# Order of loads, transposing DMAs and TensorE items in a fused sliding-window attention and MLP kernel

## The chip, the cores and the metric

The kernel runs on one core of one Trainium2 chip. The metric is the device time of one execution in microseconds. The kernel before was run four times: 331.54, 331.69, 332.9 and 333.54 us, median 332.3 us.

## What is computed

Attention with 8 batches, 8 heads, 576 positions and head size 64, in float32 at the kernel's inputs. Each query sees itself and the 127 keys before it, with a linear distance bias that depends on the head. Its output, as 4608 tokens of 512 values, goes through a two-layer MLP (512 to 2048 to 512) with the activation h / (1 + exp(-beta h)).

```python
scores = scale * np.matmul(q, k.transpose(0, 1, 3, 2))
bias = slopes[:, None, None] * (-np.abs(rel).astype(np.float32))[None, :, :]
mask = (rel >= 0) & (rel < window)          # window 128
scores = np.where(mask, scores + bias[None], -1000000000.0)
attn = softmax(scores)                      # with 1e-09 in the divisor
x = matmul(attn, v) as tokens               # (8 * 576, 512)
h = x @ w_in
g = h * (1.0 / (1.0 + np.exp(-beta * h)))
out = g @ w_out
```

## The kernel before, in words

All matmuls are in bfloat16. The work comes in small steps, each a function.

Attention, for batch b: a batch has five blocks of queries or keys (four of 128 rows and a tail of 64), and its heads go in four pairs p. For batches 0 to 2, `load_pair` (L101) brings q and k of two heads from HBM to `fst` tiles (SP's queue, L109) and GpSimd casts them into a `bst` tile (L113); `load_tail` (L117) does the same for the last 64 rows of all heads (loads L95, casts L119). `TP` and `TT` (L220, L234) transpose these on TensorE into the tile `qkT`. For batches 3 to 7, `load_qk` (L123) brings one block of q and k for all heads (loads L95 on SP, casts L129 on GpSimd) and `TD` (L245) transposes it with two transposing DMAs on SP's queue (L248). `load_v` (L134) brings a block of v: for batches 0 to 2 a load on SP and a cast (L142), for later ones a casting DMA that GpSimd issues (L137). `SC(b, m, p)` (L257) forms the scores of a pair in one half m and their exponentials (matmuls L285, ScalarE L293 or L298, VectorE mask L302). Half m = 0 needs key blocks 0 and 1 (queries up to row 383), half 1 the other three. `PV(b, qb, g)` (L314) multiplies with v for four heads of query block qb (L325, L329) and divides (VectorE L334, L335), into the tile `xn`. `X(b, qb)` (L341) puts the block, transposed, into the tile `XT`, a ring of 1536 tokens: by TensorE and a copy for batches 0 to 2 (L353, L358), by a transposing DMA on SP's queue for later ones (L349).

MLP, in nine groups g of 512 tokens: `HS(g, j)` (L363) makes one of 16 blocks of hidden values (four matmuls L372, ScalarE tanh L377, VectorE L378, into the tile `gT`); `OS(g, i, n)` (L382) adds a quarter n of the second product for 128 tokens i (four matmuls L388); with n = 3 it also scales the result on ScalarE (L403) and queues the store, which GpSimd issues two items later (L406). Below, H items and O items are calls of these.

TensorE's order is written out by hand. Batch 0 comes first; `by_pair(b)` lists the steps of batches 1 and 2, `by_block(b)` those of batches 3 to 7. `spread(moe, todo, lead, goals)` calls the list `moe` of H and O items one by one and the attention steps `todo` between them, in even measure, from item `lead` on. Batch 1 (list `s1`) runs beside group 0's items 6 to 15, batch 2 (list `s2`) beside groups 0 and 1, and later batches beside group g's H items, which alternate with the O items of group g-1 and the first three of group g.

SP's and GpSimd's orders follow from program order too. For batches 2 to 7 `merge` sets it: it gives each load, cast, TD, v load and each X of batches 3 to 7 (the list `lazy`) a place among TensorE's steps, and sorts. `first[b]` is the place of batch b's first step. A queue works in order: an instruction that waits holds those behind it. SP's queue holds loads, TD and X; GpSimd's holds casts, v loads and stores.

Of the kernel before, what the change touches and what calls it, by code (L numbers as in the profile page):

```python
# [17 lines left out]
def kernel(  # L18
# [28 lines left out]
    NTG = T // TOKG  # L47
# [69 lines left out]
    def load_tail(b):  # L117
        for i, src in enumerate((q, k)):
            nc.gpsimd.tensor_copy(  # L119
                out=tails[b % 2][0 : S - LM, i], in_=load_rows(src, b, NQB - 1)  # L120
            )
# [307 lines left out]
    def spread(moe, todo, lead, goals):  # L429
        sums = [0]  # L430
        for f in todo:
            sums.append(sums[-1] + cost.get(f, 0))
        goals = [(m, sums[n]) for m, n in goals]
        m0, w0, k = lead, 0, 0
        slope = None
        for i, it in enumerate(moe):
            flush()
            it()
            while goals and (slope is None or i + 1 >= m1):

                if slope is not None:
                    m0, w0 = m1, w1
                    goals = [g for g in goals if g[0] > m0]
                    if not goals:
                        break
                slope, m1, w1 = max(((w - w0) / (m - m0), m, w) for m, w in goals)
            w = w0 + slope * (i + 1 - m0)
            while k < len(todo) and (sums[k] + sums[k + 1]) / 2 <= min(w, w1):
                todo[k]()
                k += 1  # L450
        for f in todo[k:]:
            f()

    def step(f, c):
        cost[f] = c
        return f
# [17 lines left out]
    def pv(b, qb, g):  # L474
        return step(lambda: PV(b, qb, g), 1)
# [12 lines left out]
    def merge(steps, first):  # L488
        jobs = []

        def vals(b, sb, t0):
            casts = []
            jobs.append((t0, lambda: casts.append(load_v(b, sb))))
            if b < NTE:
                jobs.append((t0 + 4.5, lambda: casts.pop()()))

        for sb in range(NQB):
            vals(NTE - 1, sb, 1.5 * sb)
        for b in range(NTE, B):
            for sb in range(NQB):  # L500
                casts = []
                t0 = first[b] - 25 + 4.6 * sb
                jobs.append((t0, lambda b=b, sb=sb, c=casts: c.append(load_qk(b, sb))))
                jobs.append((t0 + 4.5, lambda c=casts: c.pop()()))
                jobs.append((t0 + 8.5, lambda b=b, sb=sb: TD(b, sb)))
                vals(b, sb, first[b] - 16 + 3 * sb)
        for i, f in enumerate(steps):
            if f in lazy:
                jobs.append((i + 2, f))
        jobs.sort(key=lambda j: j[0])  # L510
        out = []
        for i, f in enumerate(steps):
            while jobs and jobs[0][0] <= i:
                out.append(jobs.pop(0)[1])
            if f not in lazy:
                out.append(f)
        return out + [j[1] for j in jobs]
# [39 lines left out]
    with tc.manual_schedule(engines={mybir.EngineType.PE}):  # L557

        for sb in range(NQB):
            c = load_v(0, sb)()  # L560
            if sb in (1, 3):
                with tc.issue_after(c.ins):
                    for n in ((0,), (1, 2))[sb // 2]:
                        load_w1(n)
        for p in range(NP):
            c = load_pair(1, p, None if p else VS[0][0:1, NQB - 1, 0, 0:1])
            if p == 1:
                with tc.issue_after(c.ins):
                    load_w1(3)
                load_tail(1)  # L570
        for sb in range(NQB):
            c = load_v(1, sb)()
            if sb == 3:
                with tc.issue_after(c.ins):
                    for n in range(4):
                        load_w2(n)
        with tc.tile_pool(name="psum_x", bufs=2, space=bass.MemoryType.PSUM) as psum_x:
            pools = [psum_x, psum_s, psum_x]

            def sc0(m, p, fill=0):  # L580
                SC(0, m, p, pools[0], fill)
                pools.append(pools.pop(0))

            w = psum_t.tile([P, 512], F32, name="w", tag="t")
            idle(w[:], 9)
            TP(0, 0, 0)
            c = TP(0, 0, 1)
            with tc.issue_after(c.ins):
                late_consts()
            sc0(0, 0, 3)  # L590
            load_beta()
            TP(0, 1, 0)
            TP(0, 1, 1)
            sc0(0, 1, 2)
            TT(0)
            TP(0, 2, 0)
            sc0(1, 0, 1)
            TP(0, 2, 1)
            sc0(1, 1)
            TP(0, 3, 0)  # L600
            sc0(0, 2)
            TP(0, 3, 1)
            sc0(1, 2)
            PV(0, 0, 0)
            sc0(0, 3)
            PV(0, 1, 0)
            sc0(1, 3)
            for qb in (2, 3):
                PV(0, qb, 0)
        psum_h = ctx.enter_context(  # L610
            tc.tile_pool(name="psum_h", bufs=2, space=bass.MemoryType.PSUM))
        def hs(g):
            return [lambda j=j: HS(g, j) for j in range(NFF)]

        h0, s1 = hs(0), by_pair(1)
        with tc.tile_pool(name="psum_z", bufs=2, space=bass.MemoryType.PSUM) as psum_z:
            spare["z"] = psum_z
            w = psum_s.tile([P, 2, 512], F32, name="w", tag="sps")  # L620
            for qb in range(NQB - 1):
                PV(0, qb, 1, (psum_z, "ops") if qb % 2 else (psum_h, "hps"))
                idle(w[:, 0, :], 1)
                if qb:
                    X(0, qb - 1)
            X(0, NQB - 2)
            for it in [
                h0[0], pv(0, 4, 0), h0[1], pv(0, 4, 1), h0[2], h0[3], x(0, 4), h0[4], h0[5],
                s1[0], h0[6], s1[1],
            ]:  # L630
                it()
            del spare["z"]
        for p in range(NP):
            load_pair(2, p)
            if p == 1:
                load_tail(2)

        with tc.tile_pool(name="psum_y", bufs=1, space=bass.MemoryType.PSUM) as psum_y:
            spare["y"] = [psum_s, psum_y]
            spread(h0[7:14], s1[2:-1], 0, [(7, len(s1) - 3)])  # L640
            del spare["y"]
        psum_o = ctx.enter_context(
            tc.tile_pool(name="psum_o", bufs=2, space=bass.MemoryType.PSUM))
        for it in s1[-1], h0[14], pv(1, 3, 1), x(1, 2), h0[15], x(1, 3):
            it()

        s2 = by_pair(2)
        for f in s2[0:2]:
            f()
        steps, first = [pv(1, 4, 1)] + s2[2:9] + [x(1, 4)] + s2[9:-1], {}  # L650
        for b in range(NTE, B):
            first[b] = len(steps)
            steps += by_block(b)
        e = B - 1
        steps += pause() + [pv(e, 2, 1), x(e, 2), pv(e, 3, 0), pv(e, 3, 1), x(e, 3)]
        steps += pause() + [pv(e, 4, 0), pv(e, 4, 1), x(e, 4)]
        with tc.manual_schedule(engines={mybir.EngineType.SP, mybir.EngineType.Pool}):


            order = [(i, n) for i in range(4) for n in range(4)]  # L660

            def os(g, order):
                return [lambda i=i, n=n: OS(g, i, n) for i, n in order]

            todo = [[]]
            for f in merge(steps, first):
                if f in visits:
                    todo.append([])
                todo[-1].append(f)
            moe = [hs(1) + os(0, order[0:12]), os(0, order[12:]), os(1, order[0:3])]  # L670
            for g in range(2, NTG):
                o = os(g - 1, order[3:]) + (os(g, order[0:3]) if g < NTG - 1 else [])
                for j, h in enumerate(hs(g)):
                    moe[-1].append(h)
                    if j % 4 == 1:
                        moe.append([])
                    moe[-1] += o[j : j + 1]
            for n, m in enumerate(moe):
                r = todo[n] if n < len(todo) else []
                if n and r:  # L680
                    r.pop(0)()
                spread(m, r, 2 if n == 0 else 1, [(len(m) - (n == 0), len(r))])
            while stores:
                flush()
            for it in os(NTG - 1, order):
                it()


# [28 lines left out]
```

## Time and profile before

| | |
|---|---|
| profiled execution, whole | 331.54 us |
| its span on the core | 329.8 us |
| TensorE matmul busy | 316.1 us, 96% |
| VectorE busy | 191.7 us, 58% |
| ScalarE busy | 214.6 us, 65% |
| GpSimd busy | 106.1 us, 32% |
| H items' matmuls (L372), O items' (L388) | 146.9 us, 144.7 us |
| bytes moved by DMA | 48.26 MB, mean 146 GB/s |
| mean granted TensorE clock | 0.998 |

All times inside the profile are counted from the start of the span. A matmul's own duration overlaps with its neighbours', so that a row of such matmuls is read from their starts. A DMA's row on SP or GpSimd is the time that its issue held the queue; the transfer lands later. Where the profile names who ended a wait, it takes the last of several semaphores; if the named engine had long been done, another one, often a DMA, ended it.

### The profile page before, as it was taken

The numbers are of one execution on the slowest core, as the hardware profiler recorded it, in microseconds if no ns is written. First come the engines' busy times: TensorE is split into PE (matmuls) and PEld (weight loads), VectorE is DVE, ScalarE is ACT, GpSimd is POOL, SyncE is SP. The second block draws the span as 40 slices with busy tenths as digits, with TensorE's granted clock in tenths as the row PEclk, the third lists the DMA queues.
The fourth block names the chain that finished last, engine by engine and source line by source line (L and its number), as shares of the span: only waits on it lengthen the run. The fifth ranks groups of instructions, "written<-read, shape, count | busy, mean of one in ns | idle before, by whom it ended". The sixth has DMA issues, their size and how long they took to land.

```text
span 329.8 us, 6197 instructions
## 1 busy us (share of the span) xinstructions
PE 316.1 (96%) x2280; PEld 153.5 (47%) x2280; DVE 191.7 (58%) x413; ACT 214.6 (65%) x416; POOL 106.1 (32%) x173
## 2 busy tenths in 40 slices
PE   7879798999999998999999999999999999999995
PEld 3445355444544444454445444444454444444442
DVE  8558468995445665666666766666665434433400
ACT  5557784886777776777777777777764444544411
POOL 6743592374554243443344234400000000010000
PEclk9999999999999999999999999999999999999999
DMA  8999999999999999999999999941122200001011
GB/s 183 246 183 270 228 234 240 218 192 181 205 189 215 151 215 182 199 181 173 188 173 179 174 193 168 149 95 51 51 69 66 56 32 32 32 34 64 33 66 64
DMA packets 138638, 48.26 MB, mean 146 GB/s; under 512 B 125664, under 2 KB 136176, under 8 KB 138608
## 3 DMA queue, kind: packets, MB, share of 16 engines
q1 hardware_dynamic: 108208, 32.19, 54.9%
q0 software_dynamic: 30224, 15.54, 32.5%
q8 instruction: 18, 0.29, 0.4%
q10 hardware_dynamic: 176, 0.14, 0.1%
q14 instruction: 12, 0.10, 0.1%
HBM read 36.71 MB, written 9.44 MB: 140 GB/s over the span
## 4 chain that ended last, share of the span: by engine, by line
PE 66%; DMA 18%; SPq 7%; POOL 3%; issue 2%; ACT 2%; DVE 1%; POOLq 0%
PE ops L388 32%; PE hps L372 28%; DMA fst<-in_v_dram 7%; DMA fst<-in_k_dram 6%; DMA fst<-in_q_dram 3%; PE sps L285 3%; SPq L109 3%; SPq L95 2%; PE pv L329 2%; SPq L248 2%; PE pv L325 1%; DMA qkT<-bst 1%; POOL vs L142 1%; ACT pt L298 1%; DVE gT L378 1%
## 5 line engine op out<-in xcount | busy, mean ns | idle before, releaser
L377 ACT ACTIVATE sig<-hps,beta_h 128x512 bf16<-128x512 f32 x144 | 99.8, 696 | 79.9 <-PE hps L372 64.9
L372 PE MATMUL hps<-XT,W 128*128 128x512 bf16 x576 | 146.9, 379 | 2.4 <-DVE gT L378 1.7
L388 PE MATMUL ops<-W,gT 128*128 128x512 bf16 x576 | 144.7, 379 | 0.1
L378 DVE SCALAR_TENSOR_TENSOR gT<-sig,hps 128x512 bf16<-128x512 bf16 x144 | 98.2, 683 | 68.3 <-ACT sig L377 68.1
L388 PEld LDWEIGHTS <-gT 128*128 128x128 bf16 x576 | 53.9, 98 | 64.1 <-issue 2.1
L372 PEld LDWEIGHTS <-W 128*128 128x128 bf16 x576 | 51.1, 97 | 53.3 <-issue 4.9
L298 ACT ACTIVATE pt<-sps,bias 128x256 bf16<-128x256 f32 (+1 forms) x192 | 72.8, 492 | 2.8 <-PE sps L285 2.8
L129 POOL CAST bst<-fst 128x512 bf16<-128x512 f32 (+1 forms) x50 | 31.5, 631 | 80.4 <-DMA fst<-in_q_dram 59.5
L302 DVE TENSOR_TENSOR pt<-pt,mask 128x1024 bf16<-128x1024 bf16 x48 | 35.2, 733 | 34.6 <-ACT pt L298 34.5
L406 POOL DMA_DIRECT2D out_dram<-osb x32 | 17.8, 557 | 91.2 <-ACT osb L403 91.0
L335 DVE TENSOR_TENSOR xn<-pv,zs 128x256 bf16<-128x256 f32 (+1 forms) x80 | 33.7, 422 | 2.5
L403 ACT ACTIVATE osb<-ops 128x512 f32<-128x512 f32 x35 | 20.9, 597 | 15.3 <-PE ops L388 15.3
L329 PE MATMUL pv<-vs,pt 128*128 128x65 bf16 x320 | 28.6, 193 | 1.3 <-POOL vs L142 0.8
L329 PEld LDWEIGHTS <-pt 128*128 128x128 bf16 x320 | 21.7, 97 | 10.6 <-issue 0.8
L325 PE MATMUL pv<-vs,pt 128*128 128x65 bf16 x256 | 24.1, 193 | 0.7 <-DVE XT L358 0.5
L325 PEld LDWEIGHTS <-pt 128*128 128x128 bf16 x256 | 19.9, 98 | 7.7 <-issue 1.3
L285 PE MATMUL sps<-qkT 64*128 64x256 bf16 (+2 forms) x320 | 21.9, 251 | 0.5 <-DMA qkT<-bst 0.5
L137 POOL DMA_DIRECT2D vs<-in_v_dram x25 | 21.4, 855 | 0.6 <-issue 0.5
L293 ACT ACTIVATE pt<-sps 128x1024 bf16<-128x1024 f32 x16 | 16.3, 1023 | 6.7 <-PE sps L285 6.0
L285 PEld LDWEIGHTS <-qkT 64*128 64x128 bf16 x320 | 11.2, 94 | 19.6 <-issue 14.8
L113 POOL CAST bst<-fst 128x512 bf16<-128x512 f32 x24 | 14.6, 620 | 17.5 <-DMA fst<-in_q_dram 11.1
L334 DVE RECIPROCAL zs<-pv 128x4 f32<-128x4 f32 (+1 forms) x80 | 14.0, 175 | 10.3 <-PE pv L329 10.1
(49 smaller groups left out, 109.6 us busy)
## 6 DMA issues: line engine op xcount, KB each, us to landing
fst<-in_q_dram SPq DMA_DIRECT2D x32, 256.0 KB, 4.8
fst<-in_k_dram SPq DMA_DIRECT2D x32, 256.0 KB, 5.5
out_dram<-osb POOLq DMA_DIRECT2D x32, 256.0 KB, 3.9
fst<-in_v_dram SPq DMA_DIRECT2D x12, 256.0 KB, 6.6
vs<-in_v_dram POOLq DMA_DIRECT2D x20, 128.0 KB, 5.9
W<-in_moe_w_in_dram POOLq DMA_DIRECT2D x4, 512.0 KB, 7.1
W<-in_moe_w_out_dram POOLq DMA_DIRECT2D x4, 512.0 KB, 13.0
fst<-in_q_dram SPq DMA_DIRECT2D x8, 128.0 KB, 5.2
```

The lines of the kernel that those rows point to most:

```text
L129: nc.gpsimd.tensor_copy(out=t[0 : ROWS[sb], i], in_=f)
L137: nc.gpsimd.dma_start(out=to, in_=v[b, :, P * sb : P * sb + ROWS[sb], :].rearrange("h p d -> p h d"))
L285: nc.tensor.matmul(o, lhsT=qk[64 * e : 64 * e + 64, 1, p, P * kb : P * kb + P], rhs=qk[64 * e : 64 * e + 64, 0, p, P * kb : P * kb + nq], ...
L298: nc.scalar.activation(out=pt[:, e, cols], in_=sps[e][:, cols], func=ACTF.Exp, scale=qscale, bias=bias[:, half, h : h + 1],)
L302: nc.vector.tensor_tensor(out=pt[:], in0=pt[:], in1=masks[m][:].rearrange("p (o c) -> p o c", o=1).broadcast_to([P, 2, 512]), op=ALU.mult,)
L325: nc.tensor.matmul(pv[:, hl, 0 : D + 1], lhsT=weights(b, qb - 1, h, 1), rhs=vs[:, qb - 1, h, 0 : D + 1], start=True, stop=False,)
L329: nc.tensor.matmul(pv[:, hl, 0 : D + 1], lhsT=weights(b, qb, h, 0), rhs=vs[:, qb, h, 0 : D + 1], start=qb == 0, stop=True,)
L335: nc.vector.tensor_tensor(out=xn[0:nq, 4 * g : 4 * g + 4, :], in0=pv[0:nq, :, 0:D], in1=zs[0:nq].broadcast_to([nq, 4, D]), op=ALU.mult,)
L372: nc.tensor.matmul(hps[:], lhsT=W1[:, c, bass.ts(j, P)], rhs=XT[:, c, c0 : c0 + TOKG], start=(c == 0), stop=(c == NDM - 1),)
L377: nc.scalar.activation(out=sig[:], in_=hps[:], func=ACTF.Tanh, scale=beta_h[:, j : j + 1])
L378: nc.vector.scalar_tensor_tensor(out=gts[g][:, j, :], in0=sig[:], scalar=1.0, in1=hps[:], op0=ALU.add, op1=ALU.mult)
L388: nc.tensor.matmul(ops_[:], lhsT=gT[:, j, i * P : i * P + P], rhs=W2[:, j, :], start=(j == 0), stop=(j == NFF - 1),)
```

## The change

- `load_tail(1)` and `load_tail(2)` are called behind all four pairs of their batch instead of behind the second.
- Batch 1's steps in `spread` begin after one H item more (lead 1 instead of 0), and PV(1,4,0), `s1[-2]`, leaves that list: it now stands behind batch 2's first two TP steps.
- In `merge`, q and k loads of batches 3 to 7 with their casts and TD start at `first[b] - 26` in distances of 4.3 steps (before: -25 and 4.6). With the added step in front, `first[b]` itself is one larger.
- In `merge`, an X of batches 3 to 7 stands one step behind its place instead of two.
- The first three O items of the last group (g = 8) are put between its H items, as for the other groups, and no longer behind all of them.

```diff
-                t0 = first[b] - 25 + 4.6 * sb
+                t0 = first[b] - 26 + 4.3 * sb
...
             if f in lazy:
-                jobs.append((i + 2, f))
+                jobs.append((i + 1, f))
...
-                load_tail(1)
+        load_tail(1)
...
         for p in range(NP):
             load_pair(2, p)
-            if p == 1:
-                load_tail(2)
+        load_tail(2)
...
-            spread(h0[7:14], s1[2:-1], 0, [(7, len(s1) - 3)])
+            spread(h0[7:14], s1[2:-2], 1, [(7, len(s1) - 4)])
...
-        steps, first = [pv(1, 4, 1)] + s2[2:9] + [x(1, 4)] + s2[9:-1], {}
+        steps, first = [s1[-2], s2[2], pv(1, 4, 1)] + s2[3:9] + [x(1, 4)] + s2[9:-1], {}
...
-                o = os(g - 1, order[3:]) + (os(g, order[0:3]) if g < NTG - 1 else [])
+                o = os(g - 1, order[3:]) + os(g, order[0:3])
...
-            for it in os(NTG - 1, order):
+            for it in os(NTG - 1, order[3:]):
                 it()
```

## Prediction

> **What bounds the kernel now.** I read section 2 of the page first. TensorE is busy in nearly every slice at full clock; only the head, a few slices before 130 us and the last slice show less.
>
> ```profile
> PE   7879798999999998999999999999999999999995
> PEclk9999999999999999999999999999999999999999
> ```
>
> TensorE's own waits come next, asked from 60 us to the end. There are three in 270 us.
>
> ```profile
> PE hps L372 <- DVE gT L378: 1.7, 2, 1.1
> PE sps L285 <- DMA qkT<-bst: 0.5, 1, 0.5
> ```
>
> TensorE's instructions in order of time give their places, the first below behind SC(3,1,0), the second at HS(3,0), the third at HS(8,15); the number in brackets is the idle time before the line.
>
> ```profile
> 98.76 0.51 PE L285 MATMUL sps<-qkT 64*128 64x64 bf16 x10 [0.45 <-DMA qkT<-bst]
> ...
> 127.28 1.03 PE L388 MATMUL ops<-W,gT 128*128 128x512 bf16 x4
> 129.40 1.02 PE L372 MATMUL hps<-XT,W 128*128 128x512 bf16 x4 [1.09 <-DVE gT L378]
> ...
> 308.43 1.89 PE L372 MATMUL hps<-XT,W 128*128 128x512 bf16 x8
> 310.95 1.02 PE L372 MATMUL hps<-XT,W 128*128 128x512 bf16 x4 [0.63 <-DVE gT L378]
> ```
>
> Four 128x512 matmuls follow each other in 0.86 us (the chain of waits), 0.216 each. So the time lost is 129.40-(127.28+0.86) = 1.26 us at HS(3,0) and 310.95-(308.43+8x0.216) = 0.79 at HS(8,15).
>
> The name DVE gT is wrong at HS(3,0). Its group reads tokens 1536 to 2047, the last of them batch 3's third block (3 x 576 + 256 = 1984), so it needs X(3,2). Here is SP's queue up to that transpose, and the tile view of XT for it:
>
> ```profile
> 110.36 3.03 SPq L349 DMA_TRANSPOSE XT<-xn  x1
> 113.50 2.50 SPq L248 DMA_TRANSPOSE qkT<-bst  x2
> 116.06 0.58 SPq L95 DMA_DIRECT2D fst<-in_q_dram  x1
> 116.70 0.68 SPq L95 DMA_DIRECT2D fst<-in_k_dram  x1
> 117.47 1.69 SPq L349 DMA_TRANSPOSE XT<-xn  x1
> 119.26 2.48 SPq L248 DMA_TRANSPOSE qkT<-bst  x2
> 121.79 0.58 SPq L95 DMA_DIRECT2D fst<-in_q_dram  x1
> 122.42 1.45 SPq L95 DMA_DIRECT2D fst<-in_k_dram  x1
> 123.97 1.47 SPq L349 DMA_TRANSPOSE XT<-xn  x1
> ...
> DMA to landing us min/median/max: 5.3/5.3/5.3
> ```
>
> X(3,2) lands at 123.97+5.3 = 129.3; HS(3,0) starts at 129.40. Its values were ready earlier: PV(3,2,1) runs at 117.9, VectorE's multiply for it ends at 120.3. The queue came 3.6 us late, with no gap between the lines: it runs without a break from 60.85 to 125.44. (The view of SP's waits names GpSimd's casts there; but the casts for the transposes at 105.16, say, end at 103.9 and 104.8, before the queue reaches them.) In that stretch stand 23 transposes and 26 loads; at the shortest of each kind (1.19 and 0.57 us by the line views of L248 and L95) with 49 gaps of 0.07 they need 27.4+14.8+3.4 = 46 us, not 64.6. The 19 us above that stand where GpSimd has just issued its own transfers (L137 loads of v, L406 stores):
>
> ```profile
> 110.28 0.69 POOL L137 DMA_DIRECT2D vs<-in_v_dram  x1
> 110.96 0.58 POOL L406 DMA_DIRECT2D out_dram<-osb  x1
> ...
> 116.97 0.56 POOL L406 DMA_DIRECT2D out_dram<-osb  x1
> ...
> 122.29 0.90 POOL L137 DMA_DIRECT2D vs<-in_v_dram  x1
> ```
>
> Behind the pair at 110.3 one transpose takes 3.03 us, behind the one at 116.97 1.69, behind the one at 122.29 a load 1.45 and X(3,2) 1.47. So up to 129.4 the end is set by SP's queue and the DMA engines, afterwards by TensorE alone, which waits once more, at HS(8,15).
>
> **Part by part.** *H8 filled with O.* Worth 0.79 us at most, since three O items of group 8 now separate its last H items. What is late next is gT(8,15). From HS(8,15)'s start to the first matmul that can use it: 1.03 (its matmuls) + 0.03 + 0.69 (ACT) + 0.03 + 0.69 (DVE) + 0.05 + 0.21 (weight load, as between 311.60 and 311.81) = 2.73 us. Work in between: 4 matmuls of H, 4 of OS(8,0,2), 3 of OS(8,0,3), 11 x 0.216 = 2.38. A new wait of 0.35 remains, the gain is 0.45 us (ends 0 and 0.79).
>
> *Tails last, for batches 1 and 2.* Before, two tail casts stand between pair 1 and pair 2 on GpSimd, and TensorE waits behind them:
>
> ```profile
> 32.42 1.17 POOL L119 CAST tail<-fst 64x512 bf16<-64x512 f32 x2
> 33.53 2.01 POOL L113 CAST bst<-fst 128x512 bf16<-128x512 f32 x3
> ...
> 34.20 0.40 PE L224 MATMUL tps<-ident,bst 128*128 128x128 bf16 x4 [1.18 <-POOL bst L113]
> ```
>
> The first pair-2 cast can run 33.53-32.42 = 1.11 us earlier, and its load is issued two places earlier. *Batch 1 one H item later* lets TensorE come 0.86 later, so this wait (1.34 lost) goes. The tails are cast after pair 3, by about 36.5, where pair 3 ended at 36.34; TT(1) stands at 38.56 now. PV(1,4,0) moved behind TP(2,0) loses the wait at 49.81 for VectorE (0.50 idle), perhaps also 0.15 and 0.36 near it: together 1 us of loss. The price is denser work: 24 steps over 6 H items, with ScalarE busy 7.8 of 10 us at 30 to 50 us; up to 1 us may come back there. Net early gain 1.3 to 2.3 us. None of it reaches the end: TensorE only comes sooner to SC(3,0,0) to (3,1,0) and HS(3,0), which wait for SP, and nothing that SP waits for between 60.85 and 125.44 is TensorE's. If that cover were gone, it would be worth these 1.3 to 2.3 us.
>
> *X right behind its values, q/k loads and transposes earlier.* In the built program SP's queue has the same order as before but for the tails, and each X still waits only for its own multiply. An earlier place in the program moves nothing on a queue that is late. What changes is GpSimd's order: casts of batch 3 to 7 move ahead of v loads and stores. The casts gain nothing (SP waited for none in that stretch); the transfers behind them are issued later. Up to X(3,2): v(4,0) goes from 93.4 behind casts that end at 96.9; v(4,3) from 106.2 behind casts that end at 110.3; v(4,4) with store 6 goes from 110.3 behind casts that end at 117.0; store 7 from 117.0 to about 122.3; v(5,0) from 122.29 behind casts that end at 129.4, hence out of the way. Eighteen transfers cost SP some 19 us, about 1 each; v(5,0) measured is (1.45-0.57)+(1.47-1.19) = 1.2. One leaves, and store 7 stands nearer, as harmful as at 117.47 (1.69-1.19 = 0.5). I take X(3,2) 0.9 us earlier; bounds 2 us earlier (the two transfers and a landing of 4.5, the shortest in the XT view, instead of 5.3) and 2.3 later (the burst of 110.36, 3.03-1.19 = 1.84, plus 0.5, now directly ahead without any relief). TensorE follows 0.9: it could itself be at HS(3,0) at 128.14. Behind 129.4 no transfer is near: qkT, XT and v land 3.9 us or more before use.
>
> The Trainium skill speaks against this term: its page DMA: Bandwidth & Descriptors, section Issuing engines are not separate DMA queues, says that transfers of all issuing engines run on the same 16 DMA engines and interleave, so that a new order of issue should win nothing. By it the sum would be 0.45 us alone. The 3.03 us row agrees that they share; it does not show that order is free.
>
> **Sum.** The profiled execution took 331.54 us (span 329.8 and 1.7 around it). 331.54-0.45-0.9 = 330.2. It is the fastest of four whose median is 332.3, 0.76 above it, and I forecast a median: 330.2+0.76 = 330.95, said as 330.9.
>
> **Rivals.** *Queue unchanged.* X(3,2) lands at 129.3 as before, since SP's order is the same: only 0.45 us, 331.85. *Queue much faster.* If the relief also falls on TD(3,4) (v(4,0) no longer beside it) and both land 2 us earlier, the early gain gets through: 2+0.45, 329.85; without any SP wait 1.34+1+0.45+1.26+0.45 = 4.5, 327.8. For it: 19 us of delay are there to be lost. Against: the number of transfers ahead falls by one only. *Slower: burst in front of X(3,2).* Store 6, v(4,4) and store 7 now fall on TD(4,4), X(3,1) and X(3,2) rather than six us earlier. At 2.3 us later X(3,2) lands at 131.6, a loss of 2.3-0.45 = 1.85, 334.15. It decides from a landing 0.45 us later than now, 129.76. Against it: these transfers also leave the transposes at 105 to 113, and what SP gains there it keeps.
>
> **Numbers.** Forecast 0.45, queue unchanged 0.25, much faster 0.20, slower 0.10. About 0.5% (1.66 us) is what a measurement of this kernel can tell from no change. Faster by more: all of the third case and 0.4 of the first (X 1.2 to 2 us earlier), 0.38; slower 0.10; the rest 0.52. Range 328.8 to 333.0: it leaves out the upper half of the slow case and the far end of the fast one.
>
> **What would show it.** Right: no wait at the pair-2 transposes near 34 us; longer waits for qkT before SC(3,..) near 86 to 99 us; HS(3,0) still waiting for X(3,2), at about 128.5; the tail gap at HS(8,15) gone and one of 0.3 to 0.4 us before OS(8,0,3)'s last matmul; no other gap after 129 us. Wrong: HS(3,0) without a wait, or its start moved by more than 2 us either way, or a new wait behind it.

## The result and the profile after

The changed kernel took 331.67 us in the median of 43 runs, the kernel before 332.42 us beside it (64 runs): ratio 0.9989, 95% interval 0.9974 to 1.0005. That is 0.4 us, within 0.5% and not to be told from no change. (The medians are over all runs, the ratio over those that are not marked as slow, so it is not their quotient.) The forecast was 330.9 us, 1.4 us below the 332.3 us it started from. The profiled execution took 330.96 us (span 329.2), 0.58 less than that of before.

TensorE's own waits from 60 us to the end, the same view as for before:

```profile
PE hps L372 <- issue: 1.9, 1, 1.9
PE sps L285 <- DMA qkT<-bst: 0.6, 1, 0.6
```

TensorE in order of time, at SC(3,1,0), at HS(3,0) and at the end of group 8; idle time stands in brackets:

```profile
97.96 0.51 PE L285 MATMUL sps<-qkT 64*128 64x64 bf16 x10 [0.64 <-DMA qkT<-bst]
...
126.49 1.03 PE L388 MATMUL ops<-W,gT 128*128 128x512 bf16 x4
129.44 1.02 PE L372 MATMUL hps<-XT,W 128*128 128x512 bf16 x4 [1.93 <-issue]
...
312.79 5.51 PE L388 MATMUL ops<-W,gT 128*128 128x512 bf16 x24
```

The gap at HS(8,15) is gone: the waits that end group 8 do not appear any more. But HS(3,0) starts at 129.44, and it started at 129.40 before. TensorE could have been there at 126.49+4x0.216 = 127.35, 0.8 us sooner than before (128.14), so all it gained earlier is lost in a longer wait: 129.44-127.35 = 2.09 us instead of 1.26. The view now calls that wait "issue", as wrongly as it said DVE gT before. The real partner is in SP's queue; its last line here is X(3,2), and the tile view of XT gives its landing:

```profile
112.73 1.25 SPq L349 DMA_TRANSPOSE XT<-xn  x1
114.09 2.51 SPq L248 DMA_TRANSPOSE qkT<-bst  x2
...
117.95 2.25 SPq L349 DMA_TRANSPOSE XT<-xn  x1
120.30 2.49 SPq L248 DMA_TRANSPOSE qkT<-bst  x2
122.84 1.35 SPq L95 DMA_DIRECT2D fst<-in_q_dram  x1
124.24 0.63 SPq L95 DMA_DIRECT2D fst<-in_k_dram  x1
124.96 2.13 SPq L349 DMA_TRANSPOSE XT<-xn  x1
...
DMA to landing us min/median/max: 4.4/4.4/4.4
```

X(3,2) is issued at 124.96, 1.0 later than before, and lands at 129.35 (before 129.31). In this pair of profiles the whole 1.0 us lies ahead: TD(3,0)'s first transpose is issued at 69.69 instead of 68.65. That start scatters (69.33 in before's second profile, 69.34 in after's), so the pair alone says little of the order behind it. From HS(3,0)'s start to the end of the issue of the last store it is 197.00 us, 197.63 before. So the profiled gain is 0.63 us behind HS(3,0), and nothing in front of it.

### The profile page after: what moved, and what is told of

Same layout as the page of the kernel before. It is cut to its first block, busy times and chain, and to the rows that moved or that the text cites. A ratio compares the mean times of both kernels' runs of the same rounds, so it can differ in the third digit from the quotient of the medians.

```text
span 329.2 us, 6197 instructions
## 1 busy us (share of the span) xinstructions
PE 316.8 (96%) x2280; PEld 154.1 (47%) x2280; DVE 191.7 (58%) x413; ACT 214.6 (65%) x416; POOL 107.5 (33%) x173
## 4 chain that ended last, share of the span: by engine, by line
PE 66%; DMA 22%; SPq 4%; POOL 3%; issue 2%; ACT 1%; DVE 1%; POOLq 0%
PE ops L388 32%; PE hps L372 28%; DMA fst<-in_q_dram 11%; DMA fst<-in_v_dram 6%; DMA fst<-in_k_dram 4%; PE sps L285 3%; PE pv L329 2%; SPq L248 2%; PE pv L325 1%; SPq L109 1%; POOL bst L129 1%; DMA qkT<-bst 1%; POOL W L191 1%; ACT pt L298 1%; SPq L95 1%
## 5 line engine op out<-in xcount | busy, mean ns | idle before, releaser
L129 POOL CAST bst<-fst 128x512 bf16<-128x512 f32 (+1 forms) x50 | 32.3, 647 | 80.6 <-DMA fst<-in_q_dram 59.6
```

The source lines that it names most:

```text
L129: nc.gpsimd.tensor_copy(out=t[0 : ROWS[sb], i], in_=f)
```

## Experiments

Ratios are to the kernel before on the same chip, with 95% intervals. "Stretch" is the time from the issue of TD(3,0)'s first transpose to that of X(3,0); "hold" the time for which TD(4,1)'s first transpose held SP's queue; "wait" what TensorE lost at HS(3,0), whatever it waited for: in e9 again X(3,2) had landed 1.2 us before the start. All are from one profile each.

| kernel | ratio | stretch | hold | X(3,2) lands | HS(3,0) | wait |
|---|---|---|---|---|---|---|
| before | 1 | 41.7 | 2.60 | 129.31 | 129.40 | 1.3 |
| before again (e0) | 1.0014 [0.9976, 1.0051] | 41.7 | 2.59 | 127.84 | 128.50 | 0 |
| e1 H8 alone | 0.9985 [0.9954, 1.0016] | 42.3 | 3.64 | 130.49 | 130.58 | 0.7 |
| e3 early part alone | 0.9988 [0.9958, 1.0019] | 42.9 | 3.62 | 130.50 | 130.59 | 1.5 |
| e13 X edit alone | 1.0032 [1.0004, 1.0061] | 42.3 | 3.62 | 131.25 | 131.34 | 1.5 |
| e9 no merge edits | 0.9967 [0.9934, 1.0] | 43.2 | 2.72 | 131.49 | 131.58 | 1.8 |
| e9 again | 0.9979 [0.995, 1.0007] | 42.6 | 2.48 | 128.55 | 129.74 | 0.4 |
| e14 t0 edit alone | 1.0058 [1.0026, 1.0089] | 45.0 | 4.28 | 131.87 | 132.01 | 2.2 |
| e2 both merge edits | 1.0065 [1.0028, 1.0102] | 44.9 | 3.96 | 131.99 | 132.08 | 2.3 |
| e12 both, again | 1.0036 [1.0005, 1.0067] | 44.4 | 4.40 | 131.40 | 131.49 | 2.9 |
| after | 0.9989 [0.9974, 1.0005] | 43.0 | 3.90 | 129.35 | 129.44 | 2.1 |
| after again | 0.9988 [0.9962, 1.0015] | 44.3 | 4.05 | 130.31 | 130.40 | 2.3 |
| e16 V(4,0) early | 0.9976 [0.9944, 1.0009] | 42.2 | 2.49 | 128.01 | 128.77 | 0 |

**The three parts alone.** e1 is before with the H8 edit, e2 with the two edits in `merge`, e3 with tails last and batch 1 later.

```diff
e1, on before:
-                o = os(g - 1, order[3:]) + (os(g, order[0:3]) if g < NTG - 1 else [])
+                o = os(g - 1, order[3:]) + os(g, order[0:3])
...
-            for it in os(NTG - 1, order):
+            for it in os(NTG - 1, order[3:]):
e2, on before:
-                t0 = first[b] - 25 + 4.6 * sb
+                t0 = first[b] - 26 + 4.3 * sb
...
-                jobs.append((i + 2, f))
+                jobs.append((i + 1, f))
e3, on before: the remaining edits of the change
```

> Only the last group's first three O items between its H items, all else as before. Theory Q (SP's queue sets the start of HS(3,0); all that the change wins ahead of it is absorbed there; only the end is won): HS(3,0) starts where it did, at 129.4 +- 1 us; the gap of 0.79 us before HS(8,15) is gone and 0.1 to 0.4 us are left inside OS(8,0,3); 0.4 to 0.7 us faster, ratio 0.998 to 0.999. Rival O (GpSimd's new order or the early part also wins, and something else gives it back in the full change): this part alone shows the same 0.4 to 0.7 us, but then e2 or e3 must win too.

> Only the two edits in merge (X one step earlier, q and k loads, casts and TD earlier), all else as before. SP's order stays, GpSimd's changes. Theory Q: X(3,2) lands at 129.3 +- 1 us, ratio 1.000 +- 0.002. Rival O (the term of my forecast): X(3,2) lands 0.9 us earlier, at 128.4, ratio 0.997. Rival S (bursts fall in front of X(3,2)): lands at 131.6, ratio 1.006.

> Only the early edits: tails last for batches 1 and 2, batch 1 one H item later, PV(1,4,0) later; all else as before. Theory Q: TensorE reaches the item before HS(3,0) 0.7 to 2 us earlier than before and waits that much longer for X(3,2): the wait of 1.26 us becomes 2 to 3 us, HS(3,0) starts at 129.4 +- 1 us, ratio 1.000 +- 0.002. Rival: early gains count, HS(3,0) starts 0.7 to 2 us earlier, ratio 0.994 to 0.998.

e1 and e3 are each 0.1 to 0.15% below before, which the intervals do not tell from nothing. In e3 the wait at HS(3,0) did not grow to 2 to 3 us as expected: it is 1.5, since TensorE had already lost 1.47 at SC(3,1,0), which waits for SP as well. e2 is slower, 2.2 us. In its profile X(3,2) lands at 131.99 and HS(3,0) starts 0.09 later. In e1 the time from HS(3,0) to the end is 197.00, in e2 197.63: the H8 fill is worth 0.63 us there and needs nothing else. So the part that I had counted as a gain costs when it stands alone.

**Does anything before HS(3,0) count?** e4 and e7 are the kernel after with eight idle matmuls, ahead of SC(2,1,0) and of SC(5,0,0).

```diff
e4:
-            SC(b, m, p, pool)
+            SC(b, m, p, pool, 8 if (b, m, p) == (2, 1, 0) else 0)
e7:
-            SC(b, m, p)
+            SC(b, m, p, fill=8 if (b, m, p) == (5, 0, 0) else 0)
```

> The changed kernel with 8 further 128x512 matmuls on zeros (8 x 0.216 = 1.73 us) in front of SC(2,1,0), near 76 us. Theory Q: TensorE has 0.8 us of slack at SC(3,1,0) and 2.1 us at HS(3,0), so the wait before HS(3,0) shrinks from 2.1 to about 0.4 us, HS(3,0) starts at 129.4 +- 1 us and the time stays: ratio to before 0.999, no more than 0.3 us above the changed kernel. Rival (TensorE sets the time there too): 1.7 us longer than the changed kernel, ratio 1.004.

> The kernel after with eight added matmuls of nothing (1.73 us of TensorE) ahead of SC(5,0,0), behind HS(3,0); the same eight ahead of SC(2,1,0), before HS(3,0), gave 1.0017 of before. Theory T: behind HS(3,0) nothing absorbs them; HS(3,0) is unchanged and the part from HS(3,0) to the end grows by 1.7 us to 198.7: ratio to before 1.003 to 1.006. Rival A (there is slack behind HS(3,0) too): the end part stays at 197.0 to 197.5, ratio 0.998 to 1.0.

e7: ratio 1.0026 [0.9979, 1.0072], and the part from HS(3,0) to the end grew to 198.76 us, by 1.76, as expected. e4: 1.0017 [0.998, 1.0053]; that part is 197.23. But HS(3,0), expected at 129.4, started at 132.52: TensorE came there 2.3 us later than in after and still waited 2.92 us, because X(3,2) landed only at 132.43, 2 to 3 us later than in after's two profiles. So in e4 as well the landing set the end; whether the added matmuls made it late or it fell so by scatter is open. The expected sign, a shorter wait, did not come, and the times of e4 and e7 do not tell them apart. That time before HS(3,0) is absorbed rests on the profiles of before and after (TensorE 0.8 us sooner, HS(3,0) at the same time), not on e4.

**The whole without the merge edits.** e9 takes the two `merge` edits back out of the kernel after.

> The kernel after, with the two edits in merge taken back (t0 = first[b] - 25 + 4.6 sb, X two steps behind its place): the kernel before with H8 filled, tails last and batch 1 later. Theory M (the merge edits cost what they cost alone, 2 us, since they bunch v loads and stores in front of X(3,1) and X(3,2)): X(3,2) lands about 2 us earlier than in after, HS(3,0) loses under 0.7 us, ratio to before 0.992 to 0.995. Rival N (the merge edits cost nothing with the early edits beside them, and alone they fell on a bad order): X(3,2) at 129 to 130.5, ratio 0.997 to 1.0.

> The kernel after, once more, as the measure for the three others on the same chip and for how far X(3,2)'s landing scatters with the same code (129.35 in its first profile). Theory Q (the end is the landing of X(3,2) and a constant): whatever the landing, HS(3,0) starts 0.09 us later and the end comes 197.0 us after that. Expected landing 129 to 131, ratio to before 0.997 to 1.001.

> The kernel after without its two edits in merge, once more, beside after on the same chip. Theory M (the merge edits make X(3,2) later, 2.2 us alone): 0.5 to 2 us faster than after. Rival N (with batch 1 one item later beside them they cost nothing): within 0.5 us of after.

e9 came out at 0.9967 and 0.9979, after at 0.9989 and 0.9988. The parts add up: 0.15 + 0.12% from e1 and e3 make 0.27%, e9 has 0.33 and 0.21. The merge edits cost 0.16% (0.5 us) by the means of these pairs, less than the 0.36 and 0.65% that e12 and e2 show without the other edits; the intervals are too wide to call these different. In none of the pairs do they gain, but that they cost anything in the whole change is not shown: the intervals of after and e9 overlap, and the profiles point neither way (X(3,2) lands at 131.49 and 128.55 in e9, at 129.35 and 130.31 in after). Theory M's 2 us is not borne out in the whole change, and a gain of 0.9 us from these edits still less.

**Which of the two merge edits.** e12 is e2 again, e13 and e14 do one edit each, on before.

> The kernel before with both edits in merge and nothing else, once more (1.0065 in its first runs). Theory M (the edits bunch GpSimd's v loads and stores, and X(3,2) lands some 2 us later): ratio to before 1.004 to 1.010, HS(3,0) waits over 2 us for X(3,2). Rival N (the first result was scatter): 0.998 to 1.002.

> The kernel before with one edit: an X of batches 3 to 7 stands one step behind its place instead of two. In SP's order X(3,1) and X(3,2) keep their places, X(3,3) gets in front of one pair of loads of batch 5; GpSimd's order stays. Theory O (order decides): X(3,2) lands as in before or up to 0.5 us earlier, ratio 0.997 to 1.001. Rival P (asking for X one step earlier makes SP wait for its values and holds what stands behind): ratio 1.002 to 1.006.

> The kernel before with one edit: t0 = first[b] - 26 + 4.3 sb. In SP's order TD(4,3) gets in front of X(3,1), and the second block of batch 5 no longer separates X(3,1) and TD(4,3); GpSimd's order becomes that of after. Theory M (GpSimd's order costs the 2 us): ratio 1.004 to 1.010, as with both edits, X(3,2) landing 2 us later than in before. Rival O (the cost of the pair comes from the X edit): 0.998 to 1.002.

(Where the expectation of e14 says TD(4,3), it is TD(4,4) that gets in front of X(3,1).) The t0 edit alone costs as much as both: 1.0058, and the same signs in the profile, a stretch of 45.0 us and a hold of 4.28. The X edit alone leaves both signs within the range of the kernels with the old order. Its 1.0032 was not expected: X(3,2) landed at 131.25, but its SP order up to there is that of before. Its profile has a half-speed clock at 34 to 38 us (last section), but so has that of e1 at 0.9985; the cause stays open. Since the intervals of e13 and e14 overlap, the times alone do not say which of the two edits costs; what singles out the t0 edit is the two signs in the profile.

**Where the t0 edit costs.** The hold separates the kernels: 2.5 to 3.6 us with the old t0 (nine profiles), 3.9 to 4.4 with the new one (ten, e16 apart). The stretch nearly does, 41.7 to 43.2 against 43.0 to 45.0; its means are 42.5 and 44.4. The hold also follows the distance: it is 3.6 us in e1, e3 and e13, where V(4,1) and store 4 are issued 2.2 to 2.3 us ahead of TD(4,1), and 2.5 to 2.7 in the other six with the old t0, where it is 3.0 to 3.1. A cleaner sign is the time from TD(4,1)'s first issue to its landing, 4.8 to 6.4 us with the old t0 and 6.9 to 9.5 with the new one. Here is what stands in front of TD(4,1) on GpSimd's queue, and TD(4,1) itself (two transposes), first in before, then in after:

```profile
93.35 0.91 POOL L137 DMA_DIRECT2D vs<-in_v_dram  x1
96.86 0.89 POOL L137 DMA_DIRECT2D vs<-in_v_dram  x1
97.74 0.57 POOL L406 DMA_DIRECT2D out_dram<-osb  x1
...
99.89 3.91 SPq L248 DMA_TRANSPOSE qkT<-bst  x2
```

```profile
97.21 1.80 POOL L137 DMA_DIRECT2D vs<-in_v_dram  x2
98.98 0.60 POOL L406 DMA_DIRECT2D out_dram<-osb  x1
...
100.03 5.29 SPq L248 DMA_TRANSPOSE qkT<-bst  x2
```

V(4,0) no longer runs at 93.35, ahead of two casts, but in one bunch with V(4,1) and store 4, and the transposes behind the bunch hold SP 1.4 us longer. TD(4,1)'s first lands at 108.59 instead of 104.81. e16 takes this one transfer out of the bunch in the kernel after and changes nothing else; e0 is before once more.

```diff
e16, on after:
-                vals(b, sb, first[b] - 16 + 3 * sb)
+                vals(b, sb, first[b] - (17.5 if (b, sb) == (4, 0) else 16) + 3 * sb)
```

> The kernel after with one v load, V(4,0), in front of two casts again, as in before, so that it no longer stands in one bunch with V(4,1) and store 4 in front of TD(4,1); SP's order is after's. Theory M (the bunch holds SP): TD(4,1)'s first transpose holds SP 2.5 to 3 us instead of 3.9 to 4.4 and lands at 104 to 107 instead of 108.6 to 111, X(3,0) is issued about 1 us earlier after TD(3,0)'s first transpose (43 us instead of 44.3), and the ratio to before falls by 0.2 to 0.4% to 0.995 to 0.9975. Rival K (SP works off a fixed amount, and later transfers take the place): TD(4,1) shorter, but X(3,2) at the same distance from TD(3,0), 59.7 to 61.8 us, ratio 0.998 to 1.0.

> The kernel before, once more, for the scatter of its SP queue. Theory Z (the profile of before was an early one): the first transpose of TD(3,0) is issued at 69.5 to 70.5 instead of 68.65, X(3,2) lands at 130.0 to 131.3 instead of 129.31, the span is about 1 us longer. Rival: 68.4 to 68.9 and 129 to 129.6 again.

```profile
92.78 0.92 POOL L137 DMA_DIRECT2D vs<-in_v_dram  x1
...
97.89 0.90 POOL L137 DMA_DIRECT2D vs<-in_v_dram  x1
98.77 0.58 POOL L406 DMA_DIRECT2D out_dram<-osb  x1
...
100.99 3.80 SPq L248 DMA_TRANSPOSE qkT<-bst  x2
```

In e16 TD(4,1) holds SP 3.80 us, its first transpose 2.49 and lands at 105.89; the stretch is 42.2 us; X(3,2) lands at 128.01, and HS(3,0) does not wait. In this one profile one v load put back brings all three signs, hold, landing and stretch, back to those of the old t0 (the stretch was 43.0 and 44.3 in after's two): the bunch is what made this stretch longer. (The pair V(4,1) and store 4 then also stands 3.1 us ahead of TD(4,1) again, instead of 1.9; that the third transfer counts beside the distance is only suggested, by e1, e3 and e13, whose pair at 2.2 to 2.3 us left the landing at 6.4 us or less.) In time it is 0.9976 [0.9944, 1.0009]; that it is faster than after is likely and not shown. e0's theory fell: before's second profile had X(3,2) at 127.84, 1.5 us earlier than the first with the same code. One landing says little; the stretch and the hold repeat to 0.1 us in these two (after's two stretches differ by 1.3).

e5 shows the same from the other side. It asks for all v loads of batches 3 to 7 twelve steps later (`first[b] - 4`), which I meant as a relief.

> The kernel after, with the v loads of batches 3 to 7 asked for 12 steps later (first[b] - 4 instead of -16); in after they land 27 to 45 us before their use, so nothing needs them earlier. Theory T (SP's transposes are held by transfers that GpSimd's queue brings in front of them, and X(3,2)'s landing sets everything behind HS(3,0)): six or seven v loads leave the stretch 78 to 125; at about 0.7 us of SP time each, X(3,2) lands 3 to 4 us earlier (125.5 to 126.5 instead of 129.35), HS(3,0) waits under 0.5 us for it (2.09 in after), and the time is 1.6 to 2.1 us below after's, no more, because TensorE then is the bound: ratio to before 0.992 to 0.995. Rival N (SP's chain is as long as its own instructions make it, and its scatter of 1.5 us has nothing to do with GpSimd): X(3,2) lands at 129 to 131, ratio 0.998 to 1.002.

It became 1% slower, 1.0104 [1.0068, 1.014]: the loads did not leave the queue, they met X(3,2). These are GpSimd's transfers just ahead of it and its issue, 3.62 us:

```profile
124.95 0.90 POOL L137 DMA_DIRECT2D vs<-in_v_dram  x1
125.84 0.58 POOL L406 DMA_DIRECT2D out_dram<-osb  x1
126.40 0.90 POOL L137 DMA_DIRECT2D vs<-in_v_dram  x1
...
127.96 3.62 SPq L349 DMA_TRANSPOSE XT<-xn  x1
```

X(3,2) landed at 135.06, and HS(3,0) lost 3.8 us. Behind it the part to the end is 198.68 us instead of 197.0, mostly since the clock was halved there up to 138 us (last section). This profiled execution is the longest of twelve, 338.68 us against a median of 336.1. My expectation counted the loads that leave a stretch and not those that enter it.

**X(3,2) ahead in SP's queue.** The other way to an earlier X(3,2) is to take loads from in front of it. e6 asks for the q and k loads of batches 5 to 7 eight steps later; e10 only for those of one block, four steps later; e11 does that in e9 instead of after, and e15 is e11 again.

```diff
e6, on after:
+                t0 = first[b] - (26 if b < 5 else 18) + 4.3 * sb
e10, on after:
+                t0 = first[b] - 26 + 4.3 * sb + (4 if (b, sb) == (5, 1) else 0)
e11, on e9:
+                t0 = first[b] - 25 + 4.6 * sb + (4 if (b, sb) == (5, 1) else 0)
```

> The kernel after, with the q and k loads of batches 5 to 7 and their transposes asked for 8 steps later, which puts the loads of batch 5 behind X(3,2) in SP's queue. Theory T: four to six loads of 0.57 to 0.65 us leave SP's queue in front of X(3,2), so that it lands 2.5 to 4 us earlier and HS(3,0) loses under 0.5 us instead of 2.09: ratio to before 0.992 to 0.995. Rival L (the later loads only move the trouble): X(3,2) earlier, but the third block of batches 5, 6 or 7 comes late at SC(b,1,0) near 148, 181 or 213 (margins in after: 5.7, 5.7, 3.9 us), at 1 to 3 us each: ratio 0.998 to 1.005.

> The kernel after, with the load of the second q and k block of batch 5 asked for four steps later, which puts these two loads (1.35 and 0.63 us of SP in after) behind X(3,2) instead of in front of it; TD(5,1) then stands close in front of TD(5,2). Theory Q: X(3,2) is issued right behind TD(4,3), some 2 us earlier, and lands at 127.0 to 127.8; HS(3,0) loses at most 0.5 us (2.09 in after), and nothing is late at the scores near 132 and 148: 1.4 to 2.1 us faster than after on the same chip, ratio to before 0.992 to 0.996. Rival R (the transfers in flight set the landing, not the place in the queue): X(3,2) lands within 0.5 us of after's, ratio as after's. Rival L (what is gained there is lost at SC(5,1,0) near 148, as with all loads moved): a wait of 1 to 4 us there, ratio 0.999 to 1.008.

> The same move of two loads of batch 5, in the kernel after without its two edits in merge; there X(3,2) also gets in front of the first block of batch 5. Theory Q: X(3,2) lands 2 to 3 us earlier than in that kernel without the move, HS(3,0) loses at most 0.5 us: ratio to before 0.990 to 0.995. Rival L: a new wait at SC(5,1,0) near 148, since four loads stand bunched behind X(3,2): ratio 0.998 to 1.006.

> Once more the fastest version: H8 filled, tails last, batch 1 later, merge as before but for the loads of the second block of batch 5, which stand behind X(3,2) (0.995 in its first runs). Theory Q: HS(3,0) does not wait for X(3,2), ratio to before 0.992 to 0.997. Rival: the first result was scatter, ratio 0.997 to 1.0, as for the kernel without the move (0.9967 and 0.9979).

(Where the expectation of e10 says TD(4,3), X(3,2) stands behind TD(4,4).) e6 got X(3,2) to 126.87 and HS(3,0) lost nothing, but it is 4% slower, 1.043 [1.0367, 1.0493]: the loads are now late for their own scores, 11.7 us of waits for qkT, rival L, though far more than that rival said. Behind three of these waits the clock was halved as well, for 3.4, 7 and 3.4 us.

```profile
PE sps L285 <- DMA qkT<-bst: 11.7, 5, 5.1
```

In e10 X(3,2) landed at 127.86, 2.45 us earlier than in after on the same chip, and HS(3,0) lost nothing. The time fell by a tenth of a per cent only (0.9977 [0.9942, 1.0013] against 0.9988): 1.3 us came back as a wait of batch 7's scores for qkT, which the profile of after does not have.

```profile
214.16 0.50 PE L285 MATMUL sps<-qkT 64*128 64x256 bf16 x6 [1.29 <-DMA qkT<-bst]
```

e11 has no such wait. X(3,2) follows TD(4,4) at once and lands at 126.29; HS(3,0), the second H line here, runs at TensorE's own pace:

```profile
118.89 2.48 SPq L248 DMA_TRANSPOSE qkT<-bst  x2
121.46 2.37 SPq L349 DMA_TRANSPOSE XT<-xn  x1
...
125.67 1.03 PE L372 MATMUL hps<-XT,W 128*128 128x512 bf16 x4
126.53 1.03 PE L388 MATMUL ops<-W,gT 128*128 128x512 bf16 x4
127.39 1.03 PE L372 MATMUL hps<-XT,W 128*128 128x512 bf16 x4
```

Its times are 330.33 us, 0.995 [0.9919, 0.9982], and again (e15) 330.78 us, 0.9986 [0.9954, 1.0017]; e15's X(3,2) lands at 127.22, without a wait. In both profiles TD(3,0) was also issued early, at 67.65 and 68.30 (69.00 and 69.63 in e9's), which the move cannot have done, since SP's order ahead of it is that of e9; so 0.7 to 2 us of the earlier landing is scatter. It is the fastest version, shown faster than before in one of two series; against e9 it is not told apart.

## Why the prediction failed

**H8 filled with O: right, somewhat larger.** 0.63 us instead of 0.45 in every profile where it can be read. The gap at HS(8,15) went, and the new wait inside OS(8,0,3) that I worked out at 0.35 us is 0.15 us: from the start of the matmul at 314.08 to the next it is that much longer than in a row of such matmuls (the weights' row there is idle 0.48 us for DVE gT). The second chain, ACT and DVE behind HS(8,15), took 2.53 us from HS(8,15)'s start to that next matmul, a little less than the 2.73 that the sum of its rows gave.

**Tails last, batch 1 later: right.** The pair-2 wait near 34 us is gone, TensorE comes to HS(3,0) 0.8 us sooner, and the start of HS(3,0) does not move: the wait there grew by the same 0.8. The net early gain was 0.8 and not 1.3 to 2.3 us, since new waits came in the denser part. Here are those of after between 30 and 40 us:

```profile
31.30 1.02 PE L372 MATMUL hps<-XT,W 128*128 128x512 bf16 x4 [0.41 <-DVE gT L378]
...
37.07 0.39 PE L285 MATMUL sps<-qkT 64*128 64x256 bf16 x4 [0.61 <-ACT qkT L229]
...
39.68 0.30 PE L329 MATMUL pv<-vs,pt 128*128 128x65 bf16 x4 [0.59 <-ACT qkT L229]
```

The sum had this at nothing, which e3's 0.9988 agrees with.

**X and loads earlier in merge: this step failed.** I took X(3,2) 0.9 us earlier. It landed at 129.35 and 130.31 in after, against 129.31 and 127.84 in before; and the two edits alone made the kernel 0.36 to 0.65% slower instead of faster (e2, e12). The order behind that number was right: the program has SP's order but for the tails, and V(4,0) "goes from 93.4 behind casts that end at 96.9". The price was wrong. I gave each of GpSimd's transfers about 1 us wherever it stands, so that a new order could only win by the one that leaves the stretch, and I asked only what comes nearer to X(3,2). The place decides: three transfers in a row behind casts that end at 97 hold TD(4,1), 25 us before X(3,2), and the stretch up to X(3,0) is about 2 us longer by the means. The gain that I saw is there as well: from X(3,0)'s issue to X(3,2)'s landing it is 16.8 us with the new t0 (seven profiles with the loads in place) against 18.0 with the old (seven), 1.2 us less. X(3,0) itself holds SP 1.25 us in those seven, 1.6 to 3.5 in the old ones. Over both parts, from TD(3,0)'s issue to X(3,2)'s landing, the means of the same profiles are 60.4 us with the old t0 and 61.2 with the new: 0.9 us later instead of 0.9 earlier. Single profiles run from 58.5 to 62.5 and from 59.7 to 62.1, so that the sign is clear of noise only in the times of the edits alone (e2, e12, e14); in the whole change, after against e9, the cost is 0.5 us by the means and not told from nothing. What the runs leave of this term is no gain. Without it the forecast's own sum is 0.45 us, with the measured 0.63 for H8 it is 0.6, and a cost of up to 0.5 on top brings it down to the measured 0.4 or below.

Of the signs named ahead, the longer wait at SC(3,1,0) came (0.64 idle, before 0.45), but e0, the same kernel as before, has 0.66 there, so it shows nothing; HS(3,0) at about 128.5 did not come. The lower bound for the landing, 4.5 us from X(3,2)'s issue as the shortest seen, was no bound: e16, e9 again and e0 have 3.6 to 3.8. And "without a break" was not quite right: SP stands idle for 0.54 us inside TD(3,0), in every profile alike, so it decides nothing.

**The rivals.** "Queue unchanged" (0.25) comes nearest: 0.4 to 0.6 us below before. Its reason, that SP's order is the same, is not the whole of it: by the means above two shifts of 1 to 2 us nearly cancel. "Burst in front of X(3,2)" named the right kind of mechanism at the wrong place. What the prediction set against this term (the Trainium skill, DMA: Bandwidth & Descriptors, section Issuing engines are not separate DMA queues: all issuing engines' transfers run on the same 16 DMA engines and interleave) made the sum 0.45 us alone, which was nearer. That a new order should therefore win nothing was the prediction's own inference, and it is not what the profiles show: e16 moves one v load by 4.4 us, and TD(4,1)'s first transpose holds SP 2.49 us instead of 3.90.

The addition of 0.76 us from the profiled run to the median was no fault: after's profiled run is 0.71 us below its median.

## What to carry to other kernels

Where the critical path runs through an in-order DMA queue, look for what other queues issue in the few us ahead of each of its instructions, along its whole unbroken stretch, not only ahead of the last. Taking one transfer out of a bunch (e16) shortened this stretch by 1 to 2 us, while moving all of one kind later (e5) made a bunch at a worse place. Before a wait of one kind is bought off, find the next bound: here TensorE's own time is only 0 to 3 us ahead of the landing, and early gains are lost in between.

## What the runs showed of the hardware

One kernel's DMA landing differs by 1.5 and 2.9 us between two profiled executions (X(3,2) in before: 129.31 and 127.84; in e9, on two chips: 131.49 and 128.55), while the end of the kernel follows HS(3,0) at 197.0 to 197.1 us wherever the H8 edit is in and nothing is added or waits behind it.

Unexpected was TensorE's clock. Behind the pair-2 wait near 34 us, of kernels without the early edits, the granted clock was 0.50 for some 3.4 us in four profiles of seven. These are e14's wait and its windows of 1 us (columns: TensorE busy, clock, DMA share, GB/s):

```profile
35.19 0.42 PE L224 MATMUL tps<-ident,bst 128*128 128x128 bf16 x4 [1.90 <-POOL bst L113]
...
35.00:36.00 1.00, 0.81 (x6) 0.72 1.29 252
36.00:37.00 1.00, 1.00 (x4) 0.50 1.25 221
37.00:38.00 1.00, 1.00 (x3) 0.50 1.21 201
38.00:39.00 1.00, 1.00 (x10) 0.58 1.24 246
```

e1, e2 and e13 show it too (idle 2.00 us there); before (1.18), e12 (1.55) and e0 (2.05) do not. H2's first item starts at 96.6 to 97.4 us with it (e1, e2, e13, e14) and at 94.7 to 94.8 without (before, e12). No profile of a kernel with the tails last shows it there, so the early edits take away a loss that the early part of before has in some executions. e5 shows it after waits of 2.51 and 3.63 us, e6 after 3.58, 2.48 and, for some 7 us, 5.09. Other waits passed without it: 2.11 us at SC(3,1,0) in e9 again, and at HS(3,0) 1.93 and 2.16 in after's two profiles, 1.99 in e14, 2.09 in e2, 2.21 in e7, 2.75 in e4 and 2.77 in e12. The Trainium skill, TensorE: Matmul & The Clock Gate, section Part 1: The HAM clock gate (the "warmup" mystery), has half clock after an idle window of about 3.4 us, in windows that run freely. That the same idle time halves the clock in one run and not in another agrees with windows that do not start with the wait; that 1.90 us of idle time were enough does not agree with a window that must be idle from end to end.

This bears on the times. Every execution's mean clock is on record, and 3.4 us at half speed lower it by 0.005. Of 157 executions of before beside the experiments, 63 have a mean of 0.995 or less and took 333.4 us on average, the others 332.0. Such executions are 10 of 12 in e2, 9 in e13, 8 in e14 and 4 in e12, but 3 of 24 in e9's two series and 12 of 44 in after. So part of what the merge edits cost alone comes with more frequent dips of the clock. It is not all: among executions above 0.995, e14 (4 executions) and e12 (8) are still 1.2 and 1.0 us above those of before on the same chip, e9's two series 0.5 to 0.6 below it. Whether a dip makes an execution long, or a late landing makes the long wait and the dip, these numbers do not tell.
